# Linear attention with two MLPs: the key decay moved from v into the masks, the state's update moved to the end of a chunk

## The chip, the cores and the metric

The kernel runs on one core of a Trainium2 chip. The metric is the device time of one execution in microseconds, taken as the median of several runs. A profile is one further execution, recorded by the hardware profiler.

## What is computed

Three stages follow each other. Linear attention with a decay per head, for 4 sequences of 768 tokens, 8 heads of 64:

```python
for t in range(S):
    state = gamma[None, :, None, None] * state + np.einsum('bhd,bhe->bhde', k[:, :, t], v[:, :, t])
    y[:, :, t] = scale * np.einsum('bhd,bhde->bhe', q[:, :, t], state)
```

Its output, taken as 3072 tokens of 512 features, goes through a first MLP, `(h * sigmoid(1.702 h)) @ w_out` with `h = x @ w_in` and 2048 hidden features, and the result through a second one of the same size whose gate is `max(h, 0) + alpha * min(h, 0)`. All is float32.

## The kernel before

**Attention in chunks.** The 3072 tokens are 24 chunks of 128, six for each sequence. In a chunk the recurrence is written as products. `att_scores` makes the scores k q of each head on TensorE (PE; `sc`, L333) in two PSUM banks, one for the even heads (s = 0) and one for the odd ones (s = 1). VectorE (DVE) multiplies each bank with the causal mask in one instruction (`a`, L344). ScalarE (ACT) scales each head's v by the decay of the key's position, gamma to the power of minus j, in eight instructions (`v`, L326). `att_out` then runs four kinds of products on PE, all through the helper `product` (L361):

- the update of the state, k times the scaled v, 8 products into columns 256 to 511 of the bank px (not in the last chunk of a sequence),
- 8 masked products of v with the right half of a (all 128 rows, 64 columns),
- 8 products of the state `diag` with q (not in the first chunk of a sequence),
- 8 masked products with the left half of a, where only 64 rows are not zero.

All but the update write both banks, px and pu. PE splits each of these float32 products in two, so the profile counts 16 for 8. PE works on them with its array divided: 128 rows by 64 columns for the update and the first masked products, 64 by 64 for the state's and the last masked ones, 64 by 128 for the scores, and the whole array for the MLPs.

DVE takes the update up (`att_state`: `t`, L398, then `diag`, L401) and scales the output by the query's decay (`att_x`, L413; for chunks from 16 on `att_x_kept`, `xl`, L442). The result goes on to the first MLP, as high and low parts (`xhi`, `xlo`) for chunks 0 to 7, by way of DRAM for chunks 8 to 15, and kept in SBUF for chunks 16 to 23.

**PSUM banks.** Chunks 4 to 15 take their four banks sc0, sc1, px, pu in turn from a ring of two (`ps_a`), so px reuses the bank of sc0 and pu that of sc1, and must wait until DVE has read the scores. Chunks 0 to 3 and 16 to 23 borrow other banks by the table EARLY.

**The MLPs.** Their products are split in a high and a low part (float32r), with 12 products of 128x128 by 512 for one step (L537, L558), later in a Strassen form (L662, L760). The weights are loaded as 64-bit words, converted by ACT and DVE (L181 to L242), stored to DRAM and loaded again as needed.

**What sets the order.** A list of jobs by half steps of the MLP says in which order the program is written out: chunks 0 to 3 before the MLP starts, 4 to 7 and 8 to 15 among the steps of the first MLP, 16 to 23 among the units of its Strassen form. One job runs `att_out`, `att_x`, then the next chunk's `att_scores`. The tile framework (called the planner here) then orders each engine's instructions itself: it takes, by its own reckoning of durations, those that are ready, in the order of the program, with some raised in priority (`tc.high_priority`: mask products, evictions, gates). Each engine runs its instructions in the order so fixed, and waits where one is not ready.

**Slots and loads.** Most SBUF tiles are slots from one list of NSLOT = 82, taken at the front and given back at the end (`take`, `give`). Loads of q, k, v and weights go through a ring of five tiles (`issue`, `done`) on SyncE's queue (SP), in one order. A chunk has two of them, `qk` and `kv`; `kv` holds k for the update and v as loaded. Chunks 1 to 3 have tiles of their own (`early`).

**The start.** `cst` holds the constants: causal masks for both s (`causal`), the key's decay (`decay_v`), the state's (`decay_c`), the query's (`decay_out`). Its first part is loaded on ACT's queue (L903). Two memsets on DVE prepare the gate's table (L911) and twelve products that warm PE up (L914, L917).

```python
v = take("v", (P, H, D))
for h in range(H):
    nc.scalar.activation(
        out=v[:, h, :], in_=vt[:, h * D:(h + 1) * D], func=AF.Copy, scale=decay_v[:, h:h + 1]
    )
```

Of the kernel before, what the change touches and what calls it, by code (L numbers as in the profile page):

```python
# [8 lines left out]
F32 = mybir.dt.float32  # L9
# [5 lines left out]
ALU = mybir.AluOpType  # L15

B, H, S, D = 4, 8, 768, 64
NT, DM, DFF = B * S, H * D, 2048
P = 128
C = 128  # L20
NP = H // 2
# [1 line left out]
CPB = S // C  # L23
NF = DFF // P
RING = 5
NSLOT = 82
HC = C // 2
NLEAD = 2 * C + H + NP
NCONST = NLEAD + NP * C
BT = 512  # L30
# [41 lines left out]
def tile_linear_attention_two_mlps(ctx: ExitStack, tc, qk, kv, w1, w2, consts, alpha, out):  # L72
# [9 lines left out]
    nc = tc.nc  # L82
    pool = lambda name, bufs, **kw: ctx.enter_context(tc.tile_pool(name=name, bufs=bufs, **kw))
    cpool = pool("const", 1)
# [10 lines left out]
    causal = cst[:, 0:2 * C].rearrange("p (f i) -> p f i", f=2)  # L95
    decay_v = cst[:, 2 * C:2 * C + H]
    decay_c = cst[:, 2 * C + H:NLEAD]
    decay_out = cst[:, NLEAD:].rearrange("p (n i) -> p n i", n=NP)
    alpha_sb = cpool.tile([P, NF], F32, name="alpha_sb")
    nalpha = cpool.tile([P, NF], F32, name="nalpha")  # L100
    diag = cpool.tile([P, NP, D], F32, name="diag")
# [11 lines left out]

    free, home = deque(range(NSLOT)), {}

    def take(name, shape=(P, 512), dtype=F32):
        i = free.popleft()
        t = spool.tile(list(shape), dtype, tag=f"s{i}", name=name)
        home[id(t)] = (i, t)
        return t  # L120

    def give(*ts):
        for t in ts:
            free.append(home.pop(id(t))[0])
# [11 lines left out]
    order, source, loaded = [], {}, {}  # L136
# [6 lines left out]
    def issue(limit=RING):  # L143
        while count["issued"] < min(len(order), count["done"] + limit):
            key = order[count["issued"]]
            src = source[key]
            t = ldpool.tile([P, 1024], F32, tag="ld", name="ld")
            dst = t.bitcast(src.dtype)
            if len(src.shape) == 3:
                dst = dst.rearrange("p (a b) -> p a b", a=src.shape[1])  # L150
            nc.sync.dma_start(out=dst, in_=src)
            if key[0] in ("qk", "kv"):
                t = (t[:, :512], t[:, 512:])
            loaded[key] = t
            count["issued"] += 1

    def done():
        count["done"] += 1
        issue()
# [154 lines left out]
    def att_psum(c, which, shape):  # L314
        early = EARLY[c] if c < BT // C else EARLY[1] if c >= 4 * BT // C else {}
        if which in early:
            tag = early[which]
            return (ps_h if tag == "h" else ps_y).tile(shape, F32, tag=tag, name=which)
        return ps_a.tile(shape, F32, tag="a", name=which)

    def att_scores(c):
        qt, kt = loaded["qk", c]
        vt = loaded["kv", c][1]
# [5 lines that stand above are left out]
        ps = [att_psum(c, f"sc{s}", [P, NP, C]) for s in range(2)]  # L329
        for p in range(NP):  # L330
            for s in range(2):
                r = slice(s * D, (s + 1) * D)
                nc.tensor.matmul(  # L333
                    out=ps[s][:, p, :],
                    lhsT=kt[r, p * C:(p + 1) * C],
                    rhs=qt[r, p * C:(p + 1) * C],
                    start=True,
                    stop=True,
                )
        a = []  # L340
        for s in range(2):
            a.append(take(f"a{s}", (P, NP, C)))
            with tc.high_priority(HG):
                nc.vector.tensor_tensor(  # L344
                    out=a[s], in0=ps[s], in1=causal[:, s:s + 1, :].to_broadcast([P, NP, C]), op=ALU.mult
                )
        att[c] = (v, a)

    def att_out(c):
        first, last = c % CPB == 0, c % CPB == CPB - 1  # L350
        v, a = att.pop(c)
        qt = loaded.pop(("qk", c))[0]
        kt = loaded.pop(("kv", c))[0]
        px = [att_psum(c, which, [P, 512]) for which in ("px", "pu")]
        pu = px[0][:, 2 * C:].rearrange("p (n d) -> p n d", n=NP)
        fresh = set()

        def product(bank, half, cols, lhsT, rhs):
            begin = (bank, half) not in fresh
            fresh.add((bank, half))  # L360
            nc.tensor.matmul(  # L361
                out=px[bank][half * D:(half + 1) * D, cols], lhsT=lhsT, rhs=rhs,
                start=begin, stop=True, skip_group_check=True,
            )

        heads = [(p, s, p % 2, s ^ p % 2, p // 2 * C) for p in range(NP) for s in range(2)]
        if not last:
            for p, s, _, _, _ in heads:
                cols = slice((2 * p + s) * D, (2 * p + s + 1) * D)
                product(0, s, slice(2 * C + p * D, 2 * C + (p + 1) * D), kt[:, cols], v[:, 2 * p + s, :])  # L370
        for p, s, bank, half, at in sorted(heads, key=lambda h: h[1]):
            product(bank, half, slice(at + HC, at + C), v[:, 2 * p + s, :], a[s][:, p, HC:])
        if not first:
            for p, s, bank, half, at in heads:
                r = slice(s * D, (s + 1) * D)
                product(bank, half, slice(at, at + C), diag[r, p, :], qt[r, p * C:(p + 1) * C])
        for p, s, bank, half, at in heads:
            r = slice(s * HC, (s + 1) * HC)
            product(bank, half, slice(at, at + HC), v[r, 2 * p + s, :], a[s][r, p, :HC])
        give(v, *a)  # L380
        if c in early:
            give(*early.pop(c))
        else:
            done()
            done()
        att[c] = px, None if last else pu
        if c != BT // C - 1:
            with tc.high_priority(HG):
                att_state(c)

    def att_state(c):
        first = c % CPB == 0
        att[c], pu = att[c]
        if pu is not None:
            src = pu
            if not first:
                src = take("t", (P, NP, D))
                nc.vector.tensor_tensor(out=src, in0=pu, in1=diag, op=ALU.add)  # L398
                give(src)
            dec = decay_c.unsqueeze(2).to_broadcast([P, NP, D])  # L400
            nc.vector.tensor_tensor(out=diag, in0=src, in1=dec, op=ALU.mult)  # L401
# [427 lines left out]
    def attention(c, s_scores, s_out, s_x, s_low):  # L829
        job(s_scores, att_scores, c, load=(("qk", c), ("kv", c)))  # L830
        job(s_out, att_out, c)
        job(s_x, att_x, c)
        if c < 2 * per:
            job(s_low, att_x_low, c)
# [12 lines left out]
    for c in range(NCH):  # L847
        if c < per:
            s = 2 * c - 2 * per - 1
        elif c < 2 * per:  # L850
            s = 2 * (c - per)
        elif c < 4 * per:
            s = ATT1 + 2 * (c - 2 * per)
        else:
            s = base + c - 4 * per
# [31 lines left out]
    for s in sorted(jobs):  # L887
        for _, _, keys in jobs[s]:
            for key in keys:
                if key[0] not in ("qk", "kv") or key[1] == 0 or key[1] >= per:  # L890
                    add(key, src_of(key))

    rank = [conv_hi, att_x_low, att_out, att_x, att_scores]

    def run(slot):
# [8 lines left out]
    for c in range(1, per):  # L904
# [2 lines left out]
            nc.sync.dma_start(out=cst[:, o:], in_=consts[:, o:])  # L907
        issue(c + 2)
    nc.sync.dma_start(out=alpha_sb, in_=alpha)
    table = take("table", (P, 1))  # L910
    nc.vector.memset(table, 0.0)  # L911
    nc.scalar.activation(out=table, in_=table, func=AF.Gelu_apprx_sigmoid)
# [134 lines left out]
```

## Time and profile before

| what | value |
| --- | --- |
| median of 3 runs | 1060.81 us (1060.52 to 1062.38) |
| the profiled execution | 1061.71 us, its span 1059.9 us |
| PE busy | 1038.3 us, 98% of the span |
| DVE busy | 849.8 us, 80% |
| ACT busy | 655.2 us, 62% |
| mean granted TensorE clock | 1.000 of full speed |

The span runs from the first to the last instruction; 1.8 us of the execution lie around it. Busy time is the time in which an engine has at least one instruction at work. PE's matmul ends are modelled, so consecutive ones can overlap in the records.

### The profile page before, as it was taken

The numbers are of one execution on the slowest core, as the hardware profiler recorded it, in microseconds if no ns is written. First come the engines' busy times: TensorE is split into PE (matmuls) and PEld (weight loads), VectorE is DVE, ScalarE is ACT, GpSimd is POOL, SyncE is SP. The second block draws the span as 40 slices with busy tenths as digits, with TensorE's granted clock in tenths as the row PEclk, the third lists the DMA queues.
The fourth block names the chain that finished last, engine by engine and source line by source line (L and its number), as shares of the span: only waits on it lengthen the run. The fifth ranks groups of instructions, "written<-read, shape, count | busy, mean of one in ns | idle before, by whom it ended". The sixth has DMA issues, their size and how long they took to land.

```text
span 1059.9 us, 17734 instructions
## 1 busy us (share of the span) xinstructions
PE 1038.3 (98%) x5980; PEld 848.0 (80%) x5980; DVE 849.8 (80%) x1602; ACT 655.2 (62%) x1344; POOL 0.2 (0%) x4
## 2 busy tenths in 40 slices
PE   8999999999999999999999999999999999999998
PEld 5688887788777888888888878778888888888886
DVE  6999945574568887898899999999786987677792
ACT  7787744454466665556786577777565765556740
POOL 0000000000000000000000000000000000000000
PEclk9999999999999999999999999999999999999999
DMA  8679969789789989999999899888686765675661
GB/s 301 219 257 366 341 232 365 242 290 338 260 304 322 358 299 329 346 332 336 314 306 337 253 323 347 308 275 278 217 270 211 233 221 172 230 253 177 201 199 60
DMA packets 154138, 292.06 MB, mean 276 GB/s; under 512 B 16448, under 2 KB 33216, under 8 KB 154048
## 3 DMA queue, kind: packets, MB, share of 16 engines
q1 hardware_dynamic: 153760, 290.66, 80.8%
q8 instruction: 48, 0.79, 0.3%
q14 instruction: 42, 0.34, 0.1%
q10 hardware_dynamic: 288, 0.27, 0.1%
HBM read 214.32 MB, written 76.55 MB: 274 GB/s over the span
## 4 chain that ended last, share of the span: by engine, by line
PE 78%; DVE 9%; DMA 7%; ACT 3%; issue 2%; SPq 1%; DVEq 0%; ACTq 0%
PE py L760 24%; PE pa L662 16%; PE py L558 16%; PE pd L662 12%; PE ph L537 7%; DMA ld<-kv 2%; DMA wcin<-wb 2%; PE px L361 2%; DVE gl L525 1%; ACT v L326 1%; PE sc L333 1%; DVE gw L517 1%; DMA hw<-wcin 1%; DVE wb L216 1%; DVE gw L677 1%
## 5 line engine op out<-in xcount | busy, mean ns | idle before, releaser
L662 PE MATMUL pa<-xo,hw 128*128 128x512 f32 x960 | 243.6, 390 | 3.8 <-ACT gw L512 2.0
L760 PE MATMUL py<-gh,yw 128*128 128x512 f32 x896 | 240.3, 390 | 1.0 <-DMA yw<-wcout 0.7
L662 PEld LDWEIGHTS pa<-xo,hw 128*128 128x128 f32 x960 | 179.4, 188 | 43.2 <-ACT gw L512 3.0
L760 PEld LDWEIGHTS py<-gh,yw 128*128 128x128 f32 x896 | 167.9, 188 | 37.2 <-DMA yw<-wcout 1.4
L525 DVE TENSOR_TENSOR gl<-gw,gh 128x512 fp32r<-128x512 f32 x224 | 150.2, 688 | 44.6 <-ACT gh L524 38.5
L662 PE MATMUL pd<-xo,hw 128*128 128x512 f32 x720 | 182.7, 390 | 0.0
L524 ACT CAST gh<-gw 128x512 fp32r<-128x512 f32 x224 | 136.2, 620 | 62.6 <-PE py L760 22.5
L662 PEld LDWEIGHTS pd<-xo,hw 128*128 128x128 f32 x720 | 134.8, 188 | 28.3
L760 PE MATMUL py<-gl,yw 128*128 128x512 f32 x448 | 138.3, 390 | 1.8 <-DVE gl L525 1.8
L760 PEld LDWEIGHTS py<-gl,yw 128*128 128x128 f32 x448 | 83.9, 188 | 19.9 <-DVE gl L525 2.6
L517 DVE SCALAR_TENSOR_TENSOR gw<-t,nalpha,gw 128x512 f32<-128x512 f32 x96 | 71.4, 748 | 12.5 <-ACT gw L516 12.3
L515 ACT ACTIVATE t<-gw 128x512 f32<-128x512 f32 x72 | 45.5, 632 | 50.3 <-DVE gw L677 46.3
L773 DVE TENSOR_TENSOR yc<-py,yc 128x512 f32<-128x512 f32 x79 | 50.9, 685 | 26.5 <-PE py L760 26.5
L326 ACT ACTIVATE v<-ld,cst 128x64 f32<-128x64 f32 x168 | 44.4, 336 | 40.1 <-DMA ld<-kv 30.3
L212 ACT CAST wb<-s 128x256 fp32r<-128x256 f32 x128 | 48.0, 404 | 33.6 <-DVE s L279 17.9
L674 ACT COPY gw<-pa 128x512 f32<-128x512 f32 x80 | 46.3, 581 | 25.5 <-PE pa L662 25.1
L677 DVE TENSOR_TENSOR gw<-pd,gw 128x512 f32<-128x512 f32 x80 | 54.9, 686 | 5.0 <-PE pd L662 4.8
L216 DVE TENSOR_TENSOR wb<-s,wb 128x256 fp32r<-128x256 f32 x128 | 50.2, 420 | 8.1 <-ACT wb L212 7.5
L537 PE MATMUL ph<-xhi,whi 128*128 128x512 f32 x128 | 51.4, 402 | 1.5 <-ACT xhi L419 1.1
L558 PE MATMUL py<-gh,whi 128*128 128x512 f32 x128 | 51.2, 400 | 0.5 <-ACT gh L524 0.5
L558 PE MATMUL py<-gh,wlo 128*128 128x512 f32 x128 | 50.1, 392 | 0.0
L537 PE MATMUL ph<-xhi,wlo 128*128 128x512 f32 x128 | 50.1, 391 | 0.0
(100 smaller groups left out, 1608.9 us busy)
## 6 DMA issues: line engine op xcount, KB each, us to landing
hw<-wcin SPq DMA_DIRECT2D x280, 256.0 KB, 4.5
yw<-wcout SPq DMA_DIRECT2D x200, 256.0 KB, 3.6
ld<-w SPq DMA_DIRECT2D x64, 512.0 KB, 5.3
wcin<-wb SPq DMA_DIRECT2D x88, 256.0 KB, 5.0
wcout<-wb SPq DMA_DIRECT2D x88, 256.0 KB, 3.9
ld<-qk SPq DMA_DIRECT2D x21, 512.0 KB, 5.4
ld<-kv SPq DMA_DIRECT2D x21, 512.0 KB, 5.2
xl<-xsd SPq DMA_DIRECT2D x32, 256.0 KB, 4.8
```

Source lines behind the costliest of these rows:

```text
L212: nc.scalar.copy(out=w[:, 0:256], in_=src)
L216: nc.vector.tensor_tensor(out=w[:, 256:], in0=src, in1=w[:, 0:256].bitcast(F32), op=ALU.subtract)
L326: nc.scalar.activation(out=v[:, h, :], in_=vt[:, h * D:(h + 1) * D], func=AF.Copy, scale=decay_v[:, h:h + 1])
L517: nc.vector.scalar_tensor_tensor(out=g, in0=t, scalar=nalpha[:, ft:ft + 1], in1=g, op0=ALU.mult, op1=ALU.add)
L524: nc.scalar.copy(out=gh, in_=g)
L525: nc.vector.tensor_tensor(out=gl, in0=g, in1=gh.bitcast(F32), op=ALU.subtract)
L537: nc.tensor.matmul(out=ph, lhsT=w[:, k * P:(k + 1) * P], rhs=x[:, k, :], start=(n == 0), stop=(n == len(prods) - 1),)
L558: nc.tensor.matmul(out=py[e], lhsT=w, rhs=g, start=(begin and seen[e] == 1), stop=(end and seen[e] == 3))
L662: nc.tensor.matmul(out=ps, lhsT=w[:, 256 * part_ + k * P:256 * part_ + (k + 1) * P], rhs=x[2 * k + low], start=(n in (0, 1, 3) and m == 0) ...
L677: nc.vector.tensor_tensor(out=g, in0=ps, in1=g, op=ALU.add)
L760: nc.tensor.matmul(out=ps[e], lhsT=w[:, at:at + P], rhs=t, start=(fresh and seen[e] == 1), stop=(m == GQ - 1 and seen[e] == 3), skip_group ...
L773: add_ = lambda o, x: nc.vector.tensor_tensor(out=o, in0=ps, in1=x, op=ALU.add)
```

## The change

The key's decay goes into the masks. A new constant tile `masks` has, for each head, the causal mask with each row scaled by that head's `decay_v`; eight DVE instructions make it once at the start, written in the program ahead of the two memsets. The mask product reads it in place of `causal`. Both kinds of masked products then read v as it was loaded (`vt`) in place of the scaled v. The scaled v stays, for the state's update alone, and ACT still makes it in every chunk. From chunk 4 on the update is written last in the chunk, in chunks 0 to 3 it stays first. The masks take as much SBUF as two slots, so NSLOT goes from 82 to 80.

```diff
--- before.py
+++ after.py
@@ -23,7 +23,7 @@
 CPB = S // C
 NF = DFF // P
 RING = 5
-NSLOT = 82
+NSLOT = 80
 HC = C // 2
 NLEAD = 2 * C + H + NP
 NCONST = NLEAD + NP * C
@@ -96,6 +96,7 @@
     decay_v = cst[:, 2 * C:2 * C + H]
     decay_c = cst[:, 2 * C + H:NLEAD]
     decay_out = cst[:, NLEAD:].rearrange("p (n i) -> p n i", n=NP)
+    masks = cpool.tile([P, 2, NP, C], F32, name="masks")
     alpha_sb = cpool.tile([P, NF], F32, name="alpha_sb")
     nalpha = cpool.tile([P, NF], F32, name="nalpha")
     diag = cpool.tile([P, NP, D], F32, name="diag")
@@ -342,7 +343,7 @@
             a.append(take(f"a{s}", (P, NP, C)))
             with tc.high_priority(HG):
                 nc.vector.tensor_tensor(
-                    out=a[s], in0=ps[s], in1=causal[:, s:s + 1, :].to_broadcast([P, NP, C]), op=ALU.mult
+                    out=a[s], in0=ps[s], in1=masks[:, s], op=ALU.mult
                 )
         att[c] = (v, a)
 
@@ -350,7 +351,7 @@
         first, last = c % CPB == 0, c % CPB == CPB - 1
         v, a = att.pop(c)
         qt = loaded.pop(("qk", c))[0]
-        kt = loaded.pop(("kv", c))[0]
+        kt, vt = loaded.pop(("kv", c))
         px = [att_psum(c, which, [P, 512]) for which in ("px", "pu")]
         pu = px[0][:, 2 * C:].rearrange("p (n d) -> p n d", n=NP)
         fresh = set()
@@ -364,19 +365,25 @@
             )
 
         heads = [(p, s, p % 2, s ^ p % 2, p // 2 * C) for p in range(NP) for s in range(2)]
-        if not last:
+        cols = lambda p, s: slice((2 * p + s) * D, (2 * p + s + 1) * D)
+
+        def update():
             for p, s, _, _, _ in heads:
-                cols = slice((2 * p + s) * D, (2 * p + s + 1) * D)
-                product(0, s, slice(2 * C + p * D, 2 * C + (p + 1) * D), kt[:, cols], v[:, 2 * p + s, :])
+                product(0, s, slice(2 * C + p * D, 2 * C + (p + 1) * D), kt[:, cols(p, s)], v[:, 2 * p + s, :])
+
+        if c < BT // C and not last:
+            update()
         for p, s, bank, half, at in sorted(heads, key=lambda h: h[1]):
-            product(bank, half, slice(at + HC, at + C), v[:, 2 * p + s, :], a[s][:, p, HC:])
+            product(bank, half, slice(at + HC, at + C), vt[:, cols(p, s)], a[s][:, p, HC:])
         if not first:
             for p, s, bank, half, at in heads:
                 r = slice(s * D, (s + 1) * D)
                 product(bank, half, slice(at, at + C), diag[r, p, :], qt[r, p * C:(p + 1) * C])
         for p, s, bank, half, at in heads:
             r = slice(s * HC, (s + 1) * HC)
-            product(bank, half, slice(at, at + HC), v[r, 2 * p + s, :], a[s][r, p, :HC])
+            product(bank, half, slice(at, at + HC), vt[r, cols(p, s)], a[s][r, p, :HC])
+        if c >= BT // C and not last:
+            update()
         give(v, *a)
         if c in early:
             give(*early.pop(c))
@@ -907,6 +914,10 @@
             nc.sync.dma_start(out=cst[:, o:], in_=consts[:, o:])
         issue(c + 2)
     nc.sync.dma_start(out=alpha_sb, in_=alpha)
+    for h in range(H):
+        nc.vector.tensor_scalar(
+            out=masks[:, h % 2, h // 2, :], in0=causal[:, h % 2, :], scalar1=decay_v[:, h:h + 1], scalar2=None, op0=ALU.mult
+        )
     table = take("table", (P, 1))
     nc.vector.memset(table, 0.0)
     nc.scalar.activation(out=table, in_=table, func=AF.Gelu_apprx_sigmoid)
```

## Rows read from the trace of the kernel before

**Rows 1.** Page, part 1: busy us (share of the span) xinstructions of each engine.

```profile
PE 1038.3 (98%) x5980; PEld 848.0 (80%) x5980; DVE 849.8 (80%) x1602; ACT 655.2 (62%) x1344; POOL 0.2 (0%) x4
```

**Rows 2.** Table by stretches; columns: stretch, its us, PE, PEld, DVE, ACT, POOL busy.

```profile
245.00:330.00 85.00, 80.33 (x831) 64.78 (x830) 53.53 (x126) 46.41 (x123) 0.00 (x0) 1.00 0.82 294
```

**Rows 3.** Waits of PE, whole span: us in total, times, longest.

```profile
PE px L361 <- ACT v L326: 2.2, 2, 1.1
...
PE px L361 <- ACT wb L212: 1.6, 1, 1.6
...
PE px L361 <- DVE xl L442: 1.1, 1, 1.1
...
PE py L760 <- DMA yw<-wcout: 0.7, 1, 0.7
```

**Rows 4.** Timeline around chunk 12's block; columns: start us, us, engine, line, instruction.

```profile
180.06 0.68 DVE L344 TENSOR_TENSOR a<-sc,cst 128x512 f32<-128x512 f32 x1
180.17 0.41 ACT L212 CAST wb<-s 128x256 fp32r<-128x256 f32 x1 [0.76 <-DVE gl L525]
...
180.84 0.69 PE L361 MATMUL px<-v,ld 128*64 128x64 f32 x16 [1.59 <-ACT wb L212]
...
183.41 0.47 PE L361 MATMUL pu<-a,v 128*64 128x64 f32 x6
```

**Rows 5.** Timeline of PE, chunk 8's block (U, M, S, L, then the MLP).

```profile
143.75 0.69 PE L361 MATMUL px<-v,ld 128*64 128x64 f32 x16
144.27 0.22 PE L361 MATMUL px<-a,v 128*64 128x64 f32 x1
...
144.68 0.22 PE L361 MATMUL px<-a,v 128*64 128x64 f32 x1
144.84 0.33 PE L361 MATMUL px<-ld,diag 64*64 64x128 f32 x2
...
145.00 0.28 PE L361 MATMUL px<-ld,diag 64*64 64x128 f32 x2
...
145.10 0.28 PE L361 MATMUL px<-ld,diag 64*64 64x128 f32 x2
...
145.50 0.23 PE L361 MATMUL px<-a,v 64*64 64x64 f32 x2
...
145.66 0.50 PE L537 MATMUL ph<-xhi,whi 128*128 128x512 f32 x1
146.00 0.40 PE L537 MATMUL ph<-xhi,wlo 128*128 128x512 f32 x1
```

**Rows 6.** Chain of waits, 268 to 330 us, its shares by line.

```profile
by line: DMA ld<-kv 22.8%; ACT v L326 9.6%; DMA ld<-w 9.4%; DMA wcin<-wb 8.2%; issue 5.4%; ACT gw L674 4.6%; DVE wb L216 3.9%; ACT cvt L181 3.8%; DVE a L344 3.4%; DVE cvt L194 3.4%; DVE gw L677 3.2%; ACT gw L512 2.8%; DVE xl L442 2.4%; DVE 
```

**Rows 7.** Timeline around chunk 20's block.

```profile
289.14 0.69 PE L361 MATMUL px<-v,ld 128*64 128x64 f32 x16
289.20 1.28 DVE L344 TENSOR_TENSOR a<-sc,cst 128x512 f32<-128x512 f32 x2
...
289.94 0.27 PE L361 MATMUL px<-a,v 128*64 128x64 f32 x1
```

**Rows 8.** Timeline of DVE before chunk 10's block.

```profile
161.00 1.28 DVE L344 TENSOR_TENSOR a<-sc,cst 128x512 f32<-128x512 f32 x2
```

**Rows 9.** Groups by line and shape: busy us, mean ns, idle before.

```profile
L442 DVE TENSOR_TENSOR xl<-px,cst 128x128 f32<-128x128 f32 x16 | 4.4, 282 | 0.7 <-PE pu L361 0.7
...
L873 DVE TENSOR_SCALAR nalpha<-alpha_sb 128x16 f32<-128x16 f32 x1 | 0.2, 168 | 0.0
```

**Rows 10.** Timeline of the start.

```profile
0.72 0.40 ACTq L903 DMA_DIRECT2D cst<-consts  x1
...
1.21 4.88 PE L917 MATMUL idle<-warm 128*128 128x512 bf16 x12 [1.21 <-DVE warm L914]
...
7.21 1.29 DVE L344 TENSOR_TENSOR a<-sc,cst 128x512 f32<-128x512 f32 x2 [6.06 <-PE sc L333]
```

**Rows 11.** Instructions with tile cst: its DMAs, issue to landing.

```profile
DMA to landing us min/median/max: 4.5/5.1/5.7
```

## The prediction

> **What bounds the kernel now.** I read the engines' busy times first: TensorE (PE) works 1038.3 of 1059.9 us, 98%, VectorE (DVE) 80%, ScalarE (ACT) 62% [rows 1]. So PE bounds the kernel, and all its idle time is 21.6 us. The table by stretches shows 4.67 us of that in 245 to 330 us, where attention chunks 16 to 23 stand among the MLP steps [rows 2]. This edit can matter in two ways, by what it adds to PE's stream of products and by which waits stand at the head of a chunk's block. The list of PE's waits names ACT for the products of a chunk (v 2.2 us in two waits, the longest 1.1, and wb 1.6), DVE's xl once (1.1), and a weight load once (0.7) [rows 3]. In the timeline I looked at what ended the longest. Chunk 12's block starts at 180.84. The "wb" named had ended at 180.58, but DVE's first mask product of that chunk, from 180.06 for 0.68, ended at 180.74, 0.10 before [rows 4]. The code agrees: in chunks 4 to 15 px takes over the bank of sc0, which that mask product reads, so today's first product of the block waits for it whatever v does. Chunk 6, with the v wait of 1.1, has the same form.
>
> **The change, part by part.** I write M for the 8 masked products with the right half of a, S for the 8 state products, L for the 8 masked ones with the left half, U for the 8 of the update; the profile counts each twice.
>
> *The products themselves.* M and L read vt in place of v: same shapes, same type, same count. DVE's mask product reads masks in place of a broadcast causal, as many elements. Neither costs or gives anything that I can see. ACT still scales v in every chunk, also in 5, 11, 17 and 23, where nothing reads it any more.
>
> *U moves to the end in chunks 4 to 22 without 5, 11 and 17: 16 blocks.* Today the order is U, M, S, L, with U and M in one shape of PE (128 rows by 64 columns), S and L in 64 by 64. Afterwards it is M, S, L, U: one more change of shape in each block, from L to U. Its price is read from chunk 8 [rows 5]. M's last product starts at 144.68, S's first at 144.84, a step of 0.16 where pairs inside one shape follow after 0.06 or less; S's second comes 0.16 later again, where S's own step is 0.10 (145.00 to 145.10). That makes 0.10 and 0.06, and I take 0.15. The low end is the first gap alone, 0.10. The high end is the change from L to the MLP's full array: 0.10 by the same count (145.50 to 145.66), and 0.10 more as its first product lasts 0.50 and the next 0.40: 0.20. I take 0.15 as it is a change between the very two shapes concerned.
>
> [...]
>
> *Where PE is on the chain.* Followed back, the chain of waits runs through PE in the blocks of chunks 4, 6 to 10, 13 to 16 and 18. From 268 to 329 us, chunks 19 to 22, it runs through loads, ACT and DVE instead: 23% of that stretch is ld<-kv alone, and PE is not among its main parts [rows 6]. Chunk 12 stands behind a load as well, but what comes after it waits for PE, so I count it. That is 12 blocks, 12 x 0.15 = 1.8 us (1.2 to 2.4), and 4 x 0.15 = 0.6 in chunks 19 to 22.
>
> *Cover lost.* U also fills PE while M waits for a. In chunk 20, U starts at 289.14 and M at 289.94, when the first of two mask products (289.20, half of 1.28) is out [rows 7]. Moved behind, U no longer works under that wait, and it is worth 0.52 (143.75 to 144.27 [rows 5]). Chunks 21 and 22 repeat the pattern: 3 x 0.52 = 1.6. In chunk 10 the mask products run from 161.00 to 162.28 [rows 8] and today U, from 161.78 on, fills just the time to the second; I put 0.3 there. In chunk 12 the planner has put MLP products between the halves of M, so that the second starts only at 183.41 [rows 4], and can do so again: 0 to 0.5, I take 0. The 0.6 + 1.6 = 2.2 us of chunks 19 to 22 fall where PE is off the chain and idles 4.67 us in any case [rows 2]. The ends are 0 and 2.2; nearer to the row of the chain I take 0.5.
>
> *What U's end delays.* t, diag and the x from the px bank wait for that bank's last product, now U's, about 0.15 later after the block's start than L's is today; the pu bank is done some 0.6 us earlier, and DVE can start there. The next S is at least 4 us away. The tile of kv is held to the block's end, not to U's early one. SyncE (SP) issues the load into qk's tile, held by S, just before, one after the other, so 0 to 0.2 us for the loads queued behind on SP; these come a chunk ahead, and I take 0. No DMA is moved.
>
> *The masks.* Eight DVE instructions of 128x128 with one scalar per row. No row shows this form; below is 0.17 (128x16), above 0.28 (128x128 with two tensors) [rows 9]: 1.4 to 2.2 us, I take 1.8. They need the first part of consts, issued at 0.72 [rows 10] and landed 4.5 to 5.7 us after [rows 11], so from 5.3 on. DVE is idle until 7.21 [rows 10], 1.9 us of cover: 0. At the upper price 0.3 shows; with the cover gone all 1.8, because the chain runs on DVE from 10 to 25 us. Queued behind their wait on DVE are two memsets, if the planner leaves them there (a rival).
>
> *Two slots fewer.* Followed through the program, take finds at least 4 free slots, so 2 are left. A load into a slot waits for a release that is somewhat later. PE's one wait for such a load is 0.7 [rows 3], and loads are asked for six ahead: 0 to 0.7, I take 0.
>
> **Sum:** 1.8 + 0.3 + 0.5 = 2.6 us. The upper bound is 2.4 + 0.8 + 2.2 + 0.3 = 5.7. The profiled execution took 1061.71 us, 1.8 of it around its span, and would take 1064.3; the median of the runs is 0.9 below it, 1060.81, so I forecast 1063.4, with a range of its own of 1062.9 to 1066.5.
>
> **Rivals.**
> *Better order (faster).* The planner sees that M needs both halves of a, where U needed one, and puts the chunk's block behind more MLP products. Then the waits at the blocks' heads go: 1.1 (chunk 6), 1.6 (chunk 12), 1.1 (chunk 22) [rows 3], and 0.11 (289.14 + 0.69 to 289.94 [rows 7]) in three blocks, 4.1 in all. Less 1.8 for the shapes that is 1058.5. For it: the planner already did it inside chunk 12. Against it: in chunk 20 it foresaw no wait, since loads are later than it reckons. It decides where M starts over 0.3 us behind its mask product and PE does not idle before it. Chance 0.20.
> *Absorbed (no change).* A shape's change costs its gap only, 12 x 0.10 = 1.2, and the rest goes into PE's idle time: 1062.0. For it: the 4.67 us [rows 2]. It covers as well that the planner keeps U where it was. Chance 0.35.
> *Masks at the head (slower).* They stand in DVE's order ahead of the memset that starts the twelve warm-up products, which PE runs from 1.21 for 4.88 us [rows 10]. Those would start near 7.1, and all behind them 5.9 later: 1066.7. Against it: in the timeline ready work overtakes work that waits for a load (ACT converts weights ahead of chunk 2's v). Chance 0.08.
>
> **How the numbers follow.** The forecast has the remaining 0.37. A measurement of this kernel tells about 0.2%, 2.1 us, from no change. Slower by more than that: 0.37 + 0.08 = 0.45; within: 0.35; faster by more: 0.20. The range starts at the better order with a shape's lowest price (4.1 - 1.2, 1057.9) less 0.3, by which the fastest run is below the median, and ends at the masks' case: 1057.6 to 1066.7. Left out are a better order that also mends waits outside attention, and the masks' case together with the shapes.
>
> **What would show it.** Right: in chunks 8, 9 and 13 to 16 the block lasts 0.15 longer, with a step of 0.16 from L to U; in chunks 20 to 22 M waits for the mask product and U comes behind; the memsets stay at 0.8, and the masks lie between 5.3 and 7.2. Wrong: U follows L within 0.06 us, the waits of chunks 6 and 12 are gone, PE idles less than 4.67 us in chunks 16 to 23 by more than the shapes cost, or the warm-up starts after 1.3 us.

## The result and the profile after

| | before | after |
| --- | --- | --- |
| median of the runs side by side | 1061.60 us (4 runs, 1060.52 to 1062.53) | 1069.84 us (4 runs, 1068.30 to 1070.87) |
| ratio of after to before | | 1.0077, 95% interval 1.0060 to 1.0093 |
| profiled execution, its span | 1061.71 us, 1059.9 us | 1070.80 us, 1069.0 us |
| mean granted TensorE clock | 1.000 | 0.995 |

The change makes the kernel 8 us slower. The forecast was 1063.4 us with a range to 1066.7: the sign was right, and two thirds of the size were missing. The page's part 1 after the change, against [rows 1]:

```profile
PE 1046.4 (98%) x5980; PEld 853.0 (80%) x5980; DVE 849.9 (80%) x1610; ACT 654.1 (61%) x1344; POOL 0.2 (0%) x4
```

The span grew by 9.1 us, PE's busy time by 8.1, with the same number of products. So over the whole span PE waits only 1.0 us more. That is a balance: waits went in some places and came in others, as shown below. The rest is products that take longer, and the trace shows two things that go with it: more changes of shape (2.13 us for a block of attention that took 1.98), and a lower granted clock, which stood at 0.50 for 6.83 us from 17.85 and for 3.41 us from 721.00.

**The shapes.** The timeline of PE of after, chunk 8's block, to compare with [rows 5] (M, S, L, then U):

```profile
145.30 0.27 PE L362 MATMUL px<-a,ld 128*64 128x64 f32 x1
...
145.76 0.22 PE L362 MATMUL px<-a,ld 128*64 128x64 f32 x1
145.91 0.33 PE L362 MATMUL px<-ld,diag 64*64 64x128 f32 x2
...
146.57 0.23 PE L362 MATMUL px<-a,ld 64*64 64x64 f32 x2
146.59 0.23 PE L362 MATMUL pu<-a,ld 64*64 64x64 f32 x2
146.74 0.69 PE L362 MATMUL px<-v,ld 128*64 128x64 f32 x16
147.36 0.50 PE L544 MATMUL ph<-xhi,whi 128*128 128x512 f32 x1
```

From L's last pair in px to U is 0.17 us (146.57 to 146.74), the step that was forecast at 0.16; the pair in pu beside it starts at 146.59. From the block's first product to the end of its last one, the blocks of chunks 7, 8, 13 to 16 and 19 took 1.98 us before and take 2.13 after.

**The chunks 20 to 22.** In [rows 7] U stood ahead of M, and M waited for the mask product. The timeline of after, chunk 20:

```profile
292.83 1.28 DVE L345 TENSOR_TENSOR a<-sc,masks 128x512 f32<-128x512 f32 x2
...
294.23 0.27 PE L362 MATMUL px<-a,ld 128*64 128x64 f32 x1
```

The first half of the mask product is out at 293.5 (292.83 + 0.64), and M starts 0.7 behind it: it doesn't wait, because the planner has put the block further back. Chunks 20 and 21 now take 2.13 us instead of 2.67 and 2.60. The table by stretches of after, to compare with [rows 2], has PE idle for 1.20 us where it idled 4.67:

```profile
245.00:330.00 85.00, 83.80 (x849) 68.33 (x847) 54.18 (x126) 47.87 (x123) 0.00 (x0) 1.00 0.83 295
```

**The masks.** The timeline of DVE of after, at the start (its last row answers to [rows 10]):

```profile
0.80 0.06 DVE L922 MEMSET table<- 128x1 f32 x1 [0.80 <-PEq L1047]
0.89 0.27 DVE L925 MEMSET warm<- 128x256 uint32 x1
5.25 1.66 DVE L918 TENSOR_SCALAR masks<-cst 128x128 f32<-128x128 f32 x8 [4.09 <-DMA cst<-consts]
6.83 1.28 DVE L345 TENSOR_TENSOR a<-sc,masks 128x512 f32<-128x512 f32 x2
```

They take 1.66 us and stand behind both memsets. The first mask product starts right behind them (the records overlap by 0.08 us), which is earlier than before (7.21). The scores that it reads were done at 6.53, so the masks held it up by some 0.3 us; chunk 0's block starts at 8.46 all the same, and started at 8.47 before.

**Chunk 12.** The timeline of PE of after, where [rows 4] showed a wait of 1.59:

```profile
181.59 0.33 PE L362 MATMUL px<-a,ld 128*64 128x64 f32 x2 [0.63 <-DVE a L345]
182.19 0.27 PE L362 MATMUL pu<-a,ld 128*64 128x64 f32 x1 [0.27 <-DVE a L345]
...
183.76 0.39 PE L544 MATMUL ph<-xhi,whi 128*128 128x512 f32 x1
183.99 0.40 PE L544 MATMUL ph<-xhi,wlo 128*128 128x512 f32 x1
...
185.91 0.33 PE L362 MATMUL px<-v,ld 128*64 128x64 f32 x2
186.16 0.50 PE L544 MATMUL ph<-xlo,whi 128*128 128x512 f32 x1
186.60 0.33 PE L362 MATMUL px<-v,ld 128*64 128x64 f32 x2
186.85 0.49 PE L544 MATMUL ph<-xlo,whi 128*128 128x512 f32 x1
```

M waits 0.90 in all, less than before. But U comes only at 185.91, among MLP products, in seven pieces as ACT delivers v, and the block lasts 9.65 us where it lasted 3.61. PE hardly idles there and its granted clock is 1.00: from 183.19 to 209.44, between the 540th and the 600th MLP product, it is busy for 26.11 of 26.25 us with 259 products, where before took 23.91 with 267. The changes of shape can account for it. From 186.16 to 186.85 an MLP product and a pair of U take 0.69, where two MLP products in a row follow each other after 0.23 (183.76 to 183.99) and a pair inside one shape after 0.06. That is 0.40 for each piece, an estimate of 2.4 to 2.8 us for six or seven pieces, and 2.3 were lost. What v waits for stands in the chain of waits of after, 162 to 192 us (start, us, what):

```profile
166.99 6.52 DMA xsd<-x
...
174.82 5.31 DMA xsd<-y
...
180.14 5.28 DMA xsd<-x
...
185.51 0.36 ACT v L327
...
185.91 0.33 PE px L362 x2
```

ACT's v waits for a store: x of an earlier chunk going to DRAM. Nothing in the arithmetic ties the two together. They share a slot.

**Where the time is lost.** The start of the n-th MLP product (the first one is number 0) shows how late after is against before: +1.5 us at the 540th (before: 181.65 us), +3.9 at the 600th (205.56), +5.8 at the 720th (235.16), +3.6 at the 1080th (348.42), then level to 593 us, +1.9 at 622.11, +4.5 at 707.32, +8.7 at 721.23, and +8.8 to the end. The last step is a wait for a weight load. The timeline of PE of after, and a table by stretches (stretch, its us, PE, PEld, DVE, ACT and POOL busy, granted clock, DMA share, GB/s):

```profile
719.93 1.65 PE L767 MATMUL py<-gh,yw 128*128 128x512 f32 x5 [2.48 <-DMA yw<-wcout]
```

```profile
721.00:724.41 3.41, 3.41 (x10) 2.67 (x9) 0.00 (x0) 0.66 (x2) 0.00 (x0) 0.50 0.85 287
```

PE waited 2.48 us, and then ran at a granted clock of 0.50 for 3.41 us, which by an estimate from that share costs half of it, 1.7. Both together are the 4.2 us of that step. This is one execution: in the second profile of after (after_again, below) that wait is 1.46 us, at full clock, and the time lost from 593 to 721 us is 1.3, not 5.1.

### The profile page after: what moved, and what is told of

The parts are those of the page before. It is cut to its first block, busy times and chain, and to the rows that moved or that the text cites. A ratio compares the mean times of both kernels' runs of the same rounds, so it can differ in the third digit from the quotient of the medians.

```text
span 1069.0 us, 17749 instructions
## 1 busy us (share of the span) xinstructions
PE 1046.4 (98%) x5980; PEld 853.0 (80%) x5980; DVE 849.9 (80%) x1610; ACT 654.1 (61%) x1344; POOL 0.2 (0%) x4
## 4 chain that ended last, share of the span: by engine, by line
PE 75%; DMA 10%; DVE 8%; ACT 4%; issue 1%; SPq 1%; DVEq 0%; ACTq 0%
PE py L767 24%; PE pa L669 16%; PE py L565 14%; PE pd L669 12%; PE ph L544 6%; DMA xsd<-x 2%; PE px L362 2%; DMA wcin<-wb 2%; DMA wcout<-wb 1%; PE sc L334 1%; DVE gl L532 1%; DVE gw L684 1%; DMA yw<-wcout 1%; DMA xl<-xsd 1%; DMA ld<-kv 1%
## 5 line engine op out<-in xcount | busy, mean ns | idle before, releaser
L182 ACT ACTIVATE cvt<-ld 128x512 f32<-128x512 f32 x64 | 43.0, 672 | 12.4 <-DMA ld<-w 10.2
```

## The experiments

Ratios are to the kernel before, run on the same chip in the same rounds. The median of before there was 1058.28 us (for slots80, ulast82, ulast80 and masks_ufirst), 1059.71 (for after again, slots80_late, slots81 and after81) and 1059.56 (for the other four), so ratios are compared, not times. A ratio need not be the quotient of two medians. No variant leaves out a part of the computation.

| kernel | what it is | median us (runs) | ratio, 95% interval |
| --- | --- | --- | --- |
| after, again | the change | 1069.97 (5) | 1.0096, 1.0068 to 1.0124 |
| slots80 | before, 80 slots | 1065.68 (7) | 1.0065, 1.0042 to 1.0087 |
| ulast82 | before, U last, 82 slots | 1061.89 (12) | 1.0027, 1.0009 to 1.0045 |
| ulast80 | before, U last, 80 slots | 1078.84 (6) | 1.0166, 1.0127 to 1.0204 |
| masks_ufirst | after, U first | 1073.53 (6) | 1.0142, 1.0114 to 1.0170 |
| slots80_late | slots80, x32 given back after its store | 1060.73 (11) | 1.0000, 0.9982 to 1.0018 |
| slots81 | before, 81 slots | 1060.53 (11) | 1.0016, 0.9996 to 1.0037 |
| slots83 | before, 83 slots | 1063.14 (9) | 1.0036, 1.0018 to 1.0053 |
| after81 | after, 81 slots | 1062.71 (11) | 1.0020, 1.0000 to 1.0039 |
| after80_late | after, x32 given back after its store | 1062.06 (12) | 1.0032, 1.0018 to 1.0045 |
| after81_late | both | 1059.27 (12) | 1.0001, 0.9985 to 1.0016 |
| after81_late_u2 | both, and U between M and S | 1056.45 (12) | 0.9961, 0.9945 to 0.9977 |

### The parts of the change, one at a time

**slots80**: before with two slots fewer and nothing else.

```diff
-NSLOT = 82
+NSLOT = 80
```

> The kernel before with two slots fewer (NSLOT 80), nothing else. Theory A (the slots: the planner lays the later stages out anew, loads wait longer for a slot, PE waits for weights near 720 us): most of the late loss of 5.2 us comes with the slots alone, so 1065 to 1067 us, with the attention part up to 345 us within 1 us of before and a wait of 2 us or more for yw near 715. Theory B (the attention part delays everything by 3.6 us, and that shifts the loads of the later stages against each other): 1060.5 to 1062 us, no such wait.

Measured: 1.0065. The two slots that the forecast put at 0 cost some 6.9 us by themselves. Theory A's size came true, but not its place, so the size was luck: PE's waits for yw near 720 are 0.7 us in all, not 2, and the loss lies in the attention part. In the profile the kernel is 2.9 us ahead of before at the 540th MLP product (181.65 us in before) and 6.4 behind at the 600th, a loss of 9.3 in the blocks of chunks 12 and 13. It loses 2.1 more up to the 720th, gains 4.5 back up to the 1080th, and behind 345 us it loses another 1.2. The timeline of slots80, ACT and PE, then its chain of waits, then a table by stretches:

```profile
160.31 2.02 ACT L326 ACTIVATE v<-ld,cst 128x64 f32<-128x64 f32 x8 [1.51 <-DMA xsd<-x]
...
183.52 2.02 ACT L326 ACTIVATE v<-ld,cst 128x64 f32<-128x64 f32 x8 [1.97 <-DMA xsd<-x]
183.92 0.40 PE L361 MATMUL px<-v,ld 128*64 128x64 f32 x2 [3.47 <-ACT v L326]
...
192.22 0.63 PE L558 MATMUL py<-gh,wlo 128*128 128x512 f32 x1
```

```profile
174.12 4.67 DMA xsd<-y
...
178.85 4.57 DMA xsd<-x
...
183.52 0.36 ACT v L326
...
183.92 0.40 PE px L361 x2
```

```profile
184.04:194.28 10.24, 10.24 (x60) 6.29 (x62) 2.90 (x8) 4.82 (x18) 0.00 (x0) 0.50 0.43 147
245.00:330.00 85.00, 83.76 (x851) 68.41 (x850) 53.22 (x124) 46.70 (x122) 0.00 (x0) 1.00 0.84 298
```

PE waits 3.47 us for chunk 12's v, v waits for the store of x, and then the granted clock is 0.50 for 10.24 us: by the same estimate that costs 5.1. 3.5 + 5.1 = 8.6 of the 9.3 us. The half clock is visible in the products as well: the MLP product at 192.22, behind one like it, lasts 0.63; at full clock it lasts 0.40 [rows 5]. The second stretch of the table, against [rows 2], shows what else 80 slots change: with U first in every chunk, as in before, PE idles 1.24 us from 245 to 330 us in place of 4.67, about as little as in after, and chunks 20 and 21 take 1.98 us.

Why v waits is read from the program by following take and give: with 82 slots v of chunks 11 and 12 takes slots last held by a1 and a0, with 80 both take one last held by x32. `att_x` issues x32's store on SP and gives the slot back at once, so whoever takes it next must wait until that store has landed, as the lines above show. Two slots fewer shift which tile meets which, and the list is short enough there (14 free) that an x32 slot comes round after 13 and 9 takes.

**ulast82**: U last from chunk 4 on, M and L still reading the scaled v, 82 slots.

```diff
-        if not last:
+        if c < BT // C and not last:
+            update()
...
             product(bank, half, slice(at, at + HC), v[r, 2 * p + s, :], a[s][r, p, :HC])
+        if c >= BT // C and not last:
+            update()
```

> The kernel before with the update last from chunk 4 on, nothing else: decay still in v, 82 slots. The masked products read the scaled v. Theory A: the attention part loses 2 to 4 us, the later stages 0 to 1.5, so 1063 to 1066 us. Theory B: attention 2 to 4 us and the late loss with it, 1067 to 1070 us. Blocks of chunks 8, 9, 13 to 16 last 2.13 us by both (1.98 before).

Measured: 1.0027, so 2.9 us (1.0 to 4.8), the size that Theory A gave, and the blocks of chunks 8, 9, 13, 15 and 16 last 2.13 us. The forecast's sum for everything but the slots was 2.6.

This kernel also shows that an x32 is not dear to every v. With 82 slots v of chunks 10 and 14 takes one, and in the timeline of ulast82 ACT waits for the store of x with chunk 14's v for longer than slots80 did:

```profile
190.71 1.54 ACT L326 ACTIVATE v<-ld,cst 128x64 f32<-128x64 f32 x6 [5.00 <-DMA xsd<-x]
```

Chunk 14's block starts at 200.5, and PE doesn't wait for it. What counts is how soon PE needs the tile.

**ulast80**: ulast82 with `NSLOT = 80`.

> The kernel before with the update last from chunk 4 on and 80 slots, without masks. Its order from the second stage on is that of the changed kernel. Theory A and B: 1067 to 1071 us, as the changed kernel; if it is below 1066 us, the masks and the unscaled v cost something of their own.

Measured: 1.0166, runs from 1068.75 to 1080.07 us, worse than after itself and than both theories said. Four of its six runs lie near 1079 us and two near 1070; the profile (1078.89) is of the four. The slots and U's place are not simply added (0.65 + 0.27). Its timeline and its table by stretches:

```profile
186.46 0.47 PE L361 MATMUL px<-a,v 128*64 128x64 f32 x2 [4.18 <-ACT v L326]
```

```profile
184.40:208.29 23.89, 21.83 (x144) 15.34 (x145) 6.61 (x16) 7.40 (x28) 0.00 (x0) 0.50 0.41 142
```

The same wait for v, 4.18 us, and 23.89 us at half clock. Here M reads v too, so all of the block stands behind it.

**masks_ufirst**: after with U first in every chunk.

```diff
-        if c < BT // C and not last:
+        if not last:
             update()
...
-        if c >= BT // C and not last:
-            update()
```

> The changed kernel with the update first in every chunk again: masks, v as loaded and 80 slots stay. Theory A: as slots80 in the later stages, and in the attention part no change of shape, so 1065 to 1067.5 us. Theory B: the loss is the moved update's, so 1060.5 to 1063 us. The blocks of chunks 8, 9, 13 to 16 last 1.98 us as before by both.

Measured: 1.0142, a miss for both theories. It is slower than after, so U's place is not what makes after slow. Its timeline and table by stretches:

```profile
185.53 0.27 PE L362 MATMUL px<-v,ld 128*64 128x64 f32 x1 [2.17 <-ACT v L327]
```

```profile
187.43:201.08 13.65, 13.65 (x110) 10.58 (x110) 4.27 (x11) 2.68 (x10) 0.00 (x0) 0.50 0.40 137
```

Why it loses more than slots80 isn't settled. In the three profiles the time lost against before's span of 1059.9 us (5.6, 7.4, 17.2 us in slots80, masks_ufirst, ulast80) grows with the half clock's stretch (10.24, 13.65, 23.89 us), but these are three executions.

### Is it the number of slots, or the one that is met

**after_again**: the change as it is, on the chip of the next runs.

> The changed kernel itself, beside the others on one chip. 1.0077 of before by the first comparison; on the chip of slots80, where the same orders cost more, 1.008 to 1.017.

Measured: 1.0096, the loss repeats, and its profile has it in the same place: 6.1 us late at the 720th MLP product, where after was 5.8 late. The half clock near the start repeats in part (3.41 us from 18.27, where after had 6.83 from 17.85), and costs little: at the 100th MLP product (64.37 us in before) after is 1.1 us late and after_again 0.3, where after81 and after80_late, which run the same order up to there at full clock, are 0.4 and 0.3 ahead of before. So it makes some 1.5 us of after's loss and 0.6 of after_again's. Why only these two have it, the runs do not show.

**slots80_late**: slots80, and x32 goes back when its store has had time, as the stored weights do.

```diff
-        give(x32)
+        give_stored(x32)
```

> slots80, and x32's slot goes back to the list only after its store has left (give_stored in place of give), so that v of chunks 10 to 12 no longer takes a slot that a store of x still reads. Theory A1 (at 80 slots v of chunks 11 and 12 falls on the slot of an x32 whose store is queued on SP; ACT waits, PE idles at 184 us, its clock falls): no wait of v for xsd<-x near 180, no half clock there, 2 to 6 us below slots80, so 1.000 to 1.004 of before. Theory A2 (fewer slots cost everywhere, whatever tile held them): as slots80, 1.005 to 1.009.

Measured: 1.0000 (0.9982 to 1.0018). With the same 80 slots the whole loss is gone, so slots80 is not slow because slots are scarce. What went is the wait of chunk 12's v for the store of an x32, and slots81 below does away with it in another manner. The table by stretches of slots80_late, for the same stretch as above, has 117 products in place of 60, at full clock:

```profile
184.04:194.28 10.24, 9.96 (x117) 7.99 (x118) 6.61 (x17) 4.94 (x15) 0.00 (x0) 1.00 0.94 341
```

and among ACT's waits for v no store is left:

```profile
ACT v L326 <- DMA ld<-kv: 28.8, 12, 3.6
ACT v L326 <- DMA early<-kv: 1.9, 3, 0.9
ACT v L326 <- PE py L558: 1.5, 1, 1.5
ACT v L326 <- PE pu L361: 1.1, 1, 1.1
ACT v L326 <- DMA wcin<-wb: 0.6, 1, 0.6
```

The planner has changed its order too: on PE, U of chunk 12 stands in one piece again instead of among MLP products. Both come from the one line, and no run parts them. But the orders of the two kernels differ only in the first 270 us, so what makes 1.0000 of 1.0065 starts there. Whether the order that all 80-slot kernels share from 400 us on costs anything is open: from 593 to 721 us single executions of it take 1.1 us (slots80), 1.3 (after_again), 4.3 (slots80_late) and 5.1 (after) more than the one execution of before, and slots80_late has before's median all the same.

**slots81**: before with `NSLOT = 81`, where v of chunks 11 and 12 meets other tiles than x32.

> The kernel before with 81 slots. Theory A1: the slots v gets in chunks 11 and 12 were held by t and a1, not by an x32, so no long wait at 180 us: 0.998 to 1.003 of before. Theory A2: half of what slots80 costs, 1.002 to 1.005, with the wait at 184 half as long.

Measured: 1.0016 (0.9996 to 1.0037), no difference that can be told. Its profile does have a long wait at the head of chunk 12, 2.34 us at 181.64, but it is DVE's mask product that ends it (at 181.53), as in before [rows 4], and the clock stays at 1.00.

**after81**: after with `NSLOT = 81`.

> The changed kernel with 81 slots. Theory A1: only the moved update's cost is left, as in ulast82: 1.001 to 1.004 of before. Theory A2: halfway between ulast82 and the changed kernel, 1.005 to 1.010.

Measured: 1.0020 (1.0000 to 1.0039). One slot more gives back most of what the change lost; what is left agrees with U's share (1.0027 in ulast82).

**after80_late**: after with `give_stored(x32)`.

> The changed kernel with x32's slot given back after its store has left; 80 slots, masks and the update last stay. Theory A1 (v on the slot of a stored x32 is what makes 80 slots dear): no wait of v for xsd<-x near 180 us, and only the moved update's cost is left, 1.001 to 1.005 of before against 1.008 to 1.010 for the changed kernel. If the masks or the later stages at 80 slots cost something of their own, 1.006 or more.

Measured: 1.0032 (1.0018 to 1.0045). The same cure works in after with its 80 slots, and leaves U's share again. In its profile it is 0.1 us ahead of before at the 720th MLP product, where after was 5.8 late.

**after81_late**: both.

> The changed kernel with 81 slots and x32's slot given back late. 1.000 to 1.004 of before, as after81 (1.002). The reference for the next one.

Measured: 1.0001 (0.9985 to 1.0016).

**slots83**: before with one slot more.

> The kernel before with 83 slots. Theory A1: v of chunk 11 falls on a0's, of chunk 12 on an earlier v's slot, no store in the way: 0.996 to 1.002 of before. If more slots help in general (A2), 0.994 to 0.998.

Measured: 1.0036 (1.0018 to 1.0053), a miss: a slot more than before makes it slower, though by the program no x32 stands in the way of v of chunks 11 and 12. So an x32 is not the only way in which the number of slots can cost time. Its timeline of PE:

```profile
154.45 0.69 PE L361 MATMUL px<-v,ld 128*64 128x64 f32 x16 [1.87 <-DVE a L344]
...
692.10 1.36 PE L760 MATMUL py<-gh,yw 128*128 128x512 f32 x4 [3.52 <-ACT gh L524]
```

The number of slots changes the planner's order in both places. Which of these waits makes the median, no run shows.

### The shapes alone

**after81_late_u2**: after81_late with U between M and S, so that U stands beside M, which has its shape, and the block has the two shapes of before again. U still doesn't stand in front of M.

```diff
             product(bank, half, slice(at + HC, at + C), vt[:, cols(p, s)], a[s][:, p, HC:])
+        if c >= BT // C and not last:
+            update()
         if not first:
...
-        if c >= BT // C and not last:
-            update()
         give(v, *a)
```

> As after81_late, with the update between the masked products of the right half and the state's, so that it stands in their shape of PE. Theory C (the moved update costs one change of shape in 16 blocks, 0.15 us each): the blocks of chunks 8, 9, 13 to 16 last 1.98 us again, not 2.13, and the time is 1 to 3 us below after81_late. Rival D (a change of shape is hidden, the moved update's cost is that of the planner's new order): blocks as in after81_late or time within 1 us of it.

Measured: 0.9961 (0.9945 to 0.9977), and 2.8 us less than after81_late in the same rounds. 16 blocks by 0.15 are 2.4, so this is Theory C's forecast and not Rival D's. The timeline of PE of after81_late_u2, chunk 8:

```profile
143.71 0.22 PE L362 MATMUL px<-a,ld 128*64 128x64 f32 x1
143.76 0.64 PE L362 MATMUL px<-v,ld 128*64 128x64 f32 x16
144.33 0.33 PE L362 MATMUL px<-ld,diag 64*64 64x128 f32 x2
...
145.16 0.50 PE L544 MATMUL ph<-xhi,whi 128*128 128x512 f32 x1
```

U follows M after 0.05, and the block lasts 1.98 us again (2.13 in after81_late). This version is faster than both kernels. How much of its gain over before is due to the masks, to U behind M, or to the slots' return was not separated.

## Why the prediction was wrong, step by step

- *What bounds the kernel*: right. PE is busy for 98% in both, and every loss came through it.
- *U moves to the end, 1.8 us for 12 blocks*: right in kind and price. The block became 0.15 longer in after (1.98 to 2.13), by the step from L to U. Moving U beside M took it away (1.98 again in after81_late_u2). In chunk 12 the shape changed many times over, as U went in pieces among MLP products, at an estimated 0.40 for each piece. Whether 12 or 16 blocks pay can't be read from medians: the 2.8 us that moving U beside M gave back are nearer to 16 x 0.15 = 2.4 than to 1.8, but the runs of either kernel spread over more than 5 us.
- *Cover lost, 0.3 + 0.5*: not as told. In chunks 20 and 21 M doesn't wait with U behind it. The planner starts the block later, and the blocks got shorter. Between 245 and 330 us PE idles 1.20 us after the change (85 less 83.80 busy), where it idled 4.67 [rows 2]; after came into that stretch 5.8 us late and left it 3.9 late. The rival "better order" said that such waits would go, but its reason, that M needs both halves of a, is not what did most of it: slots80, which has U first, idles 1.24 us there, and ulast82, which has U last and 82 slots, idles 2.84 (one execution each). Most of it came with the number of slots. Of the waits that the rival priced, chunk 6's (1.1) is gone; chunk 12's fell from 1.59 to 0.90 in one profile of after and is 2.09 in the other; chunk 22's fell from 1.10 to 0.71.
- *The masks, 0*: right, 1.66 us against the 1.8 taken, under a load's wait. "Masks at the head" did not happen: the memset for the warm-up stayed at 0.89.
- *What U's end delays, 0*: nothing found against it.
- *Two slots fewer, "0 to 0.7, I take 0"*: **the step that failed.** slots80 puts it at 0.65%, 6.9 us (4.4 to 9.2), ten times the upper bound. I bounded it by PE's one wait for a weight load, as if a missing slot could only delay a load that was asked for well ahead. But the slots are one list for all tiles, so fewer of them also deal out other slots to the tiles that PE waits for. What v of chunk 12 got was a slot whose store was still on its way, behind others on SP's queue; the chain of after shows 5.31 us for y's store and then 5.28 for x's. The 4 free slots that I had counted are a count, and the question was who held the next one. The same program that gave that count also tells the holder, and it names a1 and a0 with 82 slots and x32 with 80. What a late v then costs differs between the kernels. In slots80 the products at the head of the block need it: 3.47 us of waiting, and by the estimate above 5.1 us of lost clock, and nothing in my sum allowed for a wait to cost more than its own length. In after the masked products read v as it was loaded, so only U comes late, in pieces, for 2.3 us, and the granted clock stays at 1.00. How the rest of after's loss of 8 to 10 us divides between the places named above is open, but giving x32 back late leaves 0.32% of it.

Added up by the runs: 0.27% for U (ulast82) and 0.65% for the slots (slots80) give 0.92%, between the two measurements of after, 0.77% and 0.96%. That agreement is luck: the same two parts alone make 1.66% in ulast80, and the slots with the masks make 1.42% in masks_ufirst. With the slots' part taken out, the change costs 1.0020 (after81) or 1.0032 (after80_late), 2 to 3 us, which is what the sum of the prediction says; after81_late, with both cures, is 1.0001, so some of U's price may be made up elsewhere, though its interval (to 1.0016) overlaps that of after81.

## What to carry to other kernels

Where tiles share one list of buffers, a smaller list is a change of order: follow take and give through the program and see whose buffer the critical tiles get, above all, for a tile that is needed soon, one that a store is still reading. A buffer that leaves by DMA should go to the end of the list only when its store has had time; here that one line made 80 slots as good as 82 (1.0000 of before, where slots80 was 1.0065). And it can pay to keep operations that divide PE's array alike side by side: moved behind another shape, the eight products here cost 0.15 us more in each block (2.13 in place of 1.98), and moved beside their like they gave it back.

## What the runs showed of the hardware that was not expected

Some waits of PE cost more than they lasted, as the granted clock stood at 0.50 behind them, and for how long differs much. After waits of 3.47, 4.18 and 2.17 us near 184 us, around the small products of attention, the clock stood at 0.50 for 10.24, 23.89 and 13.65 us (slots80, ulast80, masks_ufirst). After a wait of 2.48 us at 719.93 in after, among products of the whole array, it did so for 3.41 us, and likewise after 3.52 us at 692.10 in slots83. In these runs the length of the wait alone doesn't decide whether it falls: it fell for 3.41 us after 1.66 us at 323.36 in ulast80, 1.82 at 659.02 in after81_late and 2.06 at 711.23 in slots80_late too, and it stayed full after 2.05 us at 332.40 in after, 2.34 at 181.64 in slots81, 2.47 at 624.45 in after80_late, and 1.82 at 675.47 and 1.59 at 180.84 in before [rows 4]. In ulast80 the low clock began at 184.40, inside the wait; in slots80 it began at 184.04, 0.12 behind its end, and in masks_ufirst at 187.43, 1.90 behind. What decides between these the runs do not show.
